# Loading the decay matrix's rows in two transfers, one for each half of a chunk

## Chip, cores and metric

The kernel runs on one core of one Trainium2 chip. The metric is device microseconds of one execution, the median of several runs.

## What is computed

The reference chains three parts. The first is a state-space layer: over chunks of the sequence, for each batch and head, it builds a lower triangular decay matrix L from the products of the decays a between two positions, multiplies it into C Bᵀ, applies the result to x, and adds what the running state contributes. The second and third are feed-forward networks over all 3072 tokens.

```python
for c in range(nc):
    cum = np.cumsum(la, axis=-1)
    L = np.exp(cum[:, :, :, None] - cum[:, :, None, :]) * causal
    M = np.einsum('bhin,bhjn->bhij', Cc, Bc) * L
    y_intra = np.einsum('bhij,bhjd->bhid', M, xc)
    y_inter = np.einsum('bhin,bhnd->bhid', Cc, state) * np.exp(cum)[:, :, :, None]
    y[:, :, sl] = y_intra + y_inter
    state = decay_full[:, :, None, None] * state + np.sum(Bx, axis=2)
...
h = x @ w_in                        # 256 -> 2048, then ELU, then w_out: 2048 -> 256
h = (x @ w1) * (x @ w2) @ w3        # 256 -> 1024
return h @ w_out
```

Shapes: batch 4, 8 heads, 768 positions, head size 32, state size 16; weights are float32.

## The kernel before

The tokens are cut in six tiles of 512 columns (t) and 24 chunks of 128 positions (k, four to a tile). A chunk is computed as two halves of 64 positions, SUB = 2 and R = 64; the two halves lie on partitions 0 to 63 and 64 to 127 of one tile.

For a chunk, `at_load` brings its inputs (xbc, 128 rows of 4 KB), `at_l` the decays for L, `at_prep` makes L with one scan on VectorE (line 333) and bd from its last column on GpSimd, `at_cb` multiplies C Bᵀ (cb) on TensorE and that into L on VectorE (line 357), `at_u` makes the state st, and `at_y` the output y, which is split into the high and low parts xT of the next layer. Chunks 0 to 3 get their decays by matmuls with a selection matrix (`at_wide`). From chunk 4 on, `at_l` loads them (line 310): the decays lie in device memory as a_cut, one row of 8 heads by 64 positions (2 KB) for each half chunk, and each row is broadcast to the 64 partitions of its half. L has three buffers; the loads run two to three chunks ahead.

A feed-forward matmul is done as three (`mm3`, lines 240 to 242) with high and low parts of both operands. Weights arrive as 64-bit words in pieces of 512 KB (raw_wi for w_in, raw_wo for w_out, raw_wq, raw_wc, raw_wa, raw_wb for the rest), and are turned into high and low parts by VectorE and ScalarE (lines 146 to 148, 103, 104). `unit_a` computes h and the activation e, then g; `unit_b` sums acc_b over w_out; `unit_w` folds w3 into the last weight; `unit_c` and `unit_d` do the second network. After `unit_b` of the first tiles x2 is spilled to device memory (x2_dram, line 493).

The order is set by a table at the start, by a planner's costs and due times afterwards, and by a scheduler of the framework that orders each engine's instructions. All transfers are issued by SP, in order. Eight completion semaphores (DMAHW0 to DMAHW7) are used in turn: a transfer waits until the one eight places before it has landed. VectorE, ScalarE and TensorE also take their instructions in order, so one that waits holds up those behind it.

Of the kernel before, what the change touches and what calls it, by code (L numbers as in the profile page):

```python
# [13 lines left out]
NB, NH, S, D, N = 4, 8, 768, 32, 16  # L14
Q = 128
SUB = 2
R = Q // SUB
# [26 lines left out]
def kernel(  # L44
# [20 lines left out]
    nc = tc.nc  # L65
# [191 lines left out]
    a_cut = tc.dram_tile([NCHUNK * SUB, NH, R], F32, name="a_cut")  # L257
# [48 lines left out]
    def at_l(k):  # L306
        c = ck[k]
        c["L"] = att.tile([P, NH, R], F32, tag="L", name=f"L{k}", bufs=3)
        if k >= CPT:
            nc.sync.dma_start(c["L"].rearrange("p h s -> p (h s)"),  # L310
                              a_cut[SUB * k:SUB * k + SUB].rearrange("s h (o i) -> s o (h i)", o=1)
                              .to_broadcast([SUB, R, NH * R]))

    def at_wide(k):

# [99 lines left out]
    def phases(k):  # L415
        t, first = k // CPT, k % CPT == 0

        def p0():
            if k >= CPT:
                with tc.issue_after(loads[-1]):  # L420
                    if first and t + 1 < NTILE:
                        at_pr(t + 1)
                    if k + LOADS - 1 < NCHUNK:
                        at_l(k + LOADS - 1)
                    if k + LOADS < NCHUNK:
                        at_load(k + LOADS)
            if first and t:
                at_decay(t)
            at_prep(k)

        def p1():
            at_cb(k)

        def p2():
            at_cd(k)
            at_u(k)

        def p3():
            at_y(k)

        return [p0, p1, p2, p3]
# [214 lines left out]
    for k in range(CPT):  # L656
        at_l(k)
# [4 lines left out]
    for j in ORDER:  # L662
# [6 lines left out]
        elif isinstance(j, tuple):  # L669
            i, stage = j  # L670
# [7 lines left out]
    for k in range(CPT, CPT + LOADS):  # L678
        if k < CPT + LOADS - 1:
            at_l(k)  # L680
        at_load(k)
# [67 lines left out]
```

## Time and profile before

| | |
|---|---|
| median of 3 runs | 588.4 us (588.01 to 589.73) |
| the profiled execution | 588.74 us, its span 587.0 us |
| TensorE (PE) busy | 560.5 us, 95% of the span |
| VectorE (DVE) busy | 336.2 us, 57% |
| ScalarE (ACT) busy | 277.7 us, 47% |
| GpSimd (POOL) busy | 83.8 us, 14% |
| transfers | 52.78 MB, 90 GB/s over the span |
| loads of L | 20 of 256 KB |

TensorE is busy nearly all the time, but not evenly: over the first 130 us or so it has gaps, and from there to the end almost none. The shares over the whole span therefore say little about a change to the loads of L, and the reading goes by stages: which engine is full in a stage, and what it waits for. An issue on SP is the time in which SP hands a transfer to its queue; the landing comes later. "DMA share" is the mean busy share of 16 DMA engines. "Granted clock" is TensorE's clock as a share of 2.4 GHz.

### The profile page before, as it was taken

To read this page: it belongs to the slowest core of one execution; us is meant where nothing else is said; L and a number is where in the kernel's file an instruction comes from. 1 tells how busy PE (TensorE), PEld (TensorE's weight loads), DVE (VectorE), ACT (ScalarE), POOL (GpSimd) and SP (SyncE) were. 2 spreads that over 40 slices of the span, in tenths; PEclk is the share of its full clock that TensorE was granted. 3 is DMA by queue.
4 is the path that set the end of the run, shared out by engine and by line. 5 is a ranking of instruction groups with operands and counts; after the bars stand their busy time and mean duration, and the time that the engine had idled before them with its cause. 6 is when DMAs were issued, how large, how long until landed. Compare 5 with 4: busy or idle time off the path is not lost.

```text
span 587.0 us, 10429 instructions
## 1 busy us (share of the span) xinstructions
PE 560.5 (95%) x4436; PEld 439.8 (75%) x4436; DVE 336.2 (57%) x468; ACT 277.7 (47%) x390; POOL 83.8 (14%) x91
## 2 busy tenths in 40 slices
PE   5986799999999999999999999999999999999996
PEld 3665577767877888887788787887777778888784
DVE  6697879677675865668433335343676353335332
ACT  2294567565564655775323223232454552355222
POOL 2201114322222312253000000000021000000000
PEclk9999699999999999999999999999999999999999
DMA  8885353724453331621013031100110000010000
GB/s 297 298 242 155 124 173 111 260 101 126 137 195 96 113 127 73 214 86 58 1 50 113 1 126 37 54 37 1 58 53 1 1 1 0 1 37 2 0 1 36
DMA packets 26567, 52.78 MB, mean 90 GB/s; under 512 B 1592, under 2 KB 9784, under 8 KB 26520
## 3 DMA queue, kind: packets, MB, share of 16 engines
q1 hardware_dynamic: 26520, 52.11, 27.1%
q8 instruction: 35, 0.57, 0.4%
q14 instruction: 12, 0.10, 0.1%
HBM read 45.71 MB, written 6.39 MB: 89 GB/s over the span
## 4 chain that ended last, share of the span: by engine, by line
PE 77%; DMA 10%; DVE 6%; ACT 2%; issue 2%; POOL 1%; SPq 0%; POOLq 0%; DVEq 0%; ACTq 0%
PE ab L240 8%; PE ab L241 7%; PE ab L242 7%; DMA L<-a_cut 6%; PE acc_b L240 6%; PE acc_b L241 6%; PE h L240 6%; PE acc_b L242 6%; PE h L242 5%; PE h L241 5%; PE acc_d L240 4%; PE acc_d L241 4%; PE acc_d L242 4%; PE y L405 2%; DMA raw_wc<-in_w3t 2%
## 5 line engine op out<-in xcount | busy, mean ns | idle before, releaser
L469 DVE SCALAR_TENSOR_TENSOR e<-e,h 128x1024 f32<-128x1024 f32 x48 | 58.4, 1216 | 39.8 <-ACT e L468 39.8
L241 PE MATMUL acc_b<-g,w_out_hi 128*128 128x512 f32 x192 | 77.3, 403 | 3.8 <-DVE g L104 3.8
L240 PE MATMUL acc_b<-g,w_out_lo 128*128 128x512 f32 x192 | 77.9, 406 | 3.1 <-DVE w_out_lo L104 2.1
L240 PE MATMUL h<-xTh,w_in_lo 128*128 128x512 f32 (+1 forms) x196 | 78.1, 399 | 1.9 <-DVE e L469 1.0
L104 DVE TENSOR_TENSOR g<-e,g 128x1024 fp32r<-128x1024 f32 x48 | 61.6, 1283 | 29.0 <-ACT g L103 28.7
L242 PE MATMUL h<-xTh,w_in_hi 128*128 128x512 f32 (+1 forms) x196 | 76.2, 389 | 0.0
L241 PE MATMUL h<-xTl,w_in_hi 128*128 128x512 f32 (+1 forms) x196 | 76.2, 389 | 0.0
L242 PE MATMUL acc_b<-g,w_out_hi 128*128 128x512 f32 x192 | 76.1, 396 | 0.0
L240 PE MATMUL ab<-x2h,w 128*128 128x512 f32 x192 | 74.6, 394 | 0.7 <-ACT x2h L103 0.7
L241 PE MATMUL ab<-x2l,w 128*128 128x512 f32 x192 | 75.0, 391 | 0.0
L103 ACT CAST g<-e 128x1024 fp32r<-128x1024 f32 x48 | 50.4, 1050 | 52.0 <-DVE e L469 38.1
L242 PE MATMUL ab<-x2h,w 128*128 128x512 f32 x192 | 74.8, 389 | 0.0
L466 ACT ACTIVATE e<-h 128x1024 f32<-128x1024 f32 x48 | 49.2, 1026 | 44.2 <-PE h L242 43.0
L514 DVE TENSOR_TENSOR pa<-pa,ab 128x512 f32<-128x512 f32 x48 | 32.6, 684 | 61.2 <-ACT pa L513 61.2
L513 ACT COPY pa<-ab 128x512 f32<-128x512 f32 x48 | 27.9, 589 | 74.4 <-PE ab L242 73.5
L104 DVE TENSOR_TENSOR p<-pa,p 128x512 fp32r<-128x512 f32 x48 | 32.9, 692 | 34.2 <-ACT p L103 33.8
L468 ACT ACTIVATE e<-e 128x1024 f32<-128x1024 f32 x48 | 51.0, 1063 | 0.9
L103 ACT CAST p<-pa 128x512 fp32r<-128x512 f32 x48 | 29.8, 622 | 44.9 <-PE acc_d L242 23.3
L366 POOL TENSOR_TENSOR cd<-xbc,pr 128x256 f32<-128x256 f32 x24 | 24.7, 1028 | 173.9 <-issue 85.8
L240 PEld LDWEIGHTS acc_b<-g,w_out_lo 128*128 128x128 f32 x192 | 36.6, 190 | 13.1 <-DVE w_out_lo L104 2.5
L241 PEld LDWEIGHTS acc_b<-g,w_out_hi 128*128 128x128 f32 x192 | 36.6, 191 | 12.8 <-DVE g L104 5.2
L240 PEld LDWEIGHTS h<-xTh,w_in_lo 128*128 128x128 f32 x196 | 37.2, 190 | 11.5 <-DVE e L469 1.5
(93 smaller groups left out, 898.5 us busy)
## 6 DMA issues: line engine op xcount, KB each, us to landing
xbc<-in_xc SPq DMA_DIRECT2D x24, 512.0 KB, 9.8
raw_wc<-in_w3t SPq DMA_DIRECT2D x16, 512.0 KB, 7.0
L<-a_cut SPq DMA_DIRECT2D x20, 256.0 KB
raw_wi<-in_w_in SPq DMA_DIRECT2D x8, 512.0 KB, 11.9
raw_wo<-in_w_out SPq DMA_DIRECT2D x8, 512.0 KB
out_t<-o SPq DMA_DIRECT2D x12, 256.0 KB, 2.0
raw_wq<-in_wo SPq DMA_DIRECT2D x4, 512.0 KB, 11.5
raw_wb<-in_w SPq DMA_DIRECT2D x4, 512.0 KB
```

What stands on the lines that cost most here:

```text
L103: A.copy(hi, raw)
L104: return lo_eng.tensor_tensor(out=lo, in0=raw, in1=hi.bitcast(F32), op=ALU.subtract)
L240: last_mm[:] = [T.matmul(out, wlo, xhi, start=first, stop=False, **kw).ins]
L241: T.matmul(out, whi, xlo, start=False, stop=False, **kw)
L242: T.matmul(out, whi, xhi, start=False, stop=last, **kw)
L366: G.tensor_tensor(out=c["cd"], in0=c["cp"].rearrange("p s (w i) -> p s w i", w=2), in1=c["pr"].rearrange("p s (o i) -> p s o i", o=1).to_b ...
L405: mm = T.matmul(both[rows, s, g], state[k, s][rows, D * g:D * g + D], c["cd"][rows, s, g], start=False, stop=True, skip_group_check=True)
L466: A.activation(e, h, AF.Exp)
L468: A.activation(e, e, AF.Relu, scale=-1.0, bias=1.0)
L469: V.scalar_tensor_tensor(out=e, in0=e, scalar=-1.0, in1=h, op0=ALU.mult, op1=ALU.max)
L513: A.copy(e, h[:, 0])
L514: V.tensor_tensor(out=e, in0=e, in1=h[:, 1], op=ALU.mult)
```

## The change

`at_l` issues two transfers for a chunk in place of one. Each brings the row of one half to its 64 partitions. In the one transfer the axes were half, partition, row; in each of the two they are partition and row, so that the partitions are outermost. Bytes, destination and source are the same.

```diff
--- before.py
+++ after.py
@@ -307,9 +307,10 @@
         c = ck[k]
         c["L"] = att.tile([P, NH, R], F32, tag="L", name=f"L{k}", bufs=3)
         if k >= CPT:
-            nc.sync.dma_start(c["L"].rearrange("p h s -> p (h s)"),
-                              a_cut[SUB * k:SUB * k + SUB].rearrange("s h (o i) -> s o (h i)", o=1)
-                              .to_broadcast([SUB, R, NH * R]))
+
+            for s in range(SUB):
+                nc.sync.dma_start(c["L"][R * s:R * s + R].rearrange("p h s -> p (h s)"),
+                                  a_cut[SUB * k + s:SUB * k + s + 1].rearrange("s h i -> s (h i)").to_broadcast([R, NH * R]))
 
     def at_wide(k):
```

SP has 20 transfers more, and the semaphores that go round are taken by other transfers. On SP, from the loads of L4 and L5 on (the number behind a name is the chunk or the piece), before:

```order
L310 DMA L4_430<-a_cut_86 128x1x512 [waits DMAHW3_49,DVE_49]
L310 DMA L5_434<-a_cut_86 128x1x512 [waits DMAHW4_49,DVE_49,PE_49]
L278 DMA xbc6_438<-in_xc 128x1024 [waits DMAHW5_49,Pool_49]
L136 DMA raw_wo3_357<-in_w_out 128x2x512 [waits DMAHW6_49,DVE_49]
L136 DMA raw_wi6_442<-in_w_in 128x2x512 [waits DMAHW7_49,DVE_49]
L136 DMA raw_wo4_465<-in_w_out 128x2x512 [waits DMAHW0_49,DVE_49]
L136 DMA raw_wi7_492<-in_w_in 128x2x512 [waits DMAHW1_49,DVE_49]
L136 DMA raw_wo5_519<-in_w_out 128x2x512 [waits DMAHW2_49,DVE_49]
L294 DMA pr2_537<-in_a_h 128x1x512 [waits DMAHW3_49,Pool_49]
L310 DMA L6_539<-a_cut_86 128x1x512 [waits DMAHW4_49,PE_49]
```

and now:

```order
L312 DMA L4_430<-a_cut_86 64x512 [waits DMAHW3_49,DVE_49]
L312 DMA L4_430<-a_cut_86 64x512 [waits DMAHW4_49]
L312 DMA L5_435<-a_cut_86 64x512 [waits DMAHW5_49,DVE_49,PE_49]
L312 DMA L5_435<-a_cut_86 64x512 [waits DMAHW6_49]
L278 DMA xbc6_440<-in_xc 128x1024 [waits DMAHW7_49,Pool_49]
L136 DMA raw_wo3_357<-in_w_out 128x2x512 [waits DMAHW0_49,DVE_49]
L136 DMA raw_wi6_444<-in_w_in 128x2x512 [waits DMAHW1_49,DVE_49]
L136 DMA raw_wo4_467<-in_w_out 128x2x512 [waits DMAHW2_49,DVE_49]
L136 DMA raw_wi7_494<-in_w_in 128x2x512 [waits DMAHW3_49,DVE_49]
L136 DMA raw_wo5_521<-in_w_out 128x2x512 [waits DMAHW4_49,DVE_49]
L294 DMA pr2_539<-in_a_h 128x1x512 [waits DMAHW5_49,Pool_49]
L312 DMA L6_541<-a_cut_86 64x512 [waits DMAHW6_49,PE_49]
```

L6 waited for DMAHW4, which L5 signals. Now its first half waits for DMAHW6, which the second half of L5 signals. xbc6 waits for DMAHW7 in place of DMAHW5.

Up to about the first fold of w3 the other engines have the order of before. There SP has, before:

```order
L310 DMA L11_1208<-a_cut_86 128x1x512 [waits DMAHW6_49,DVE_49,PE_49]
L278 DMA xbc12_1210<-in_xc 128x1024 [waits DMAHW7_49,Pool_49]
L493 DMA x2_dramh_87<-x2h0_1091 128x1024 [waits DMAHW0_49,Activation_49]
L136 DMA raw_wc1_1217<-in_w3t 128x4x256 [waits DMAHW1_49]
L493 DMA x2_draml_88<-x2l0_1092 128x1024 [waits DMAHW2_49,DVE_49]
L136 DMA raw_wc2_1221<-in_w3t 128x4x256 [waits DMAHW3_49,Pool_49]
```

and now:

```order
L312 DMA L11_1215<-a_cut_86 64x512 [waits DMAHW5_49,DVE_49,PE_49]
L312 DMA L11_1215<-a_cut_86 64x512 [waits DMAHW6_49]
L494 DMA x2_dramh_87<-x2h0_1098 128x1024 [waits DMAHW7_49,Activation_49]
L494 DMA x2_draml_88<-x2l0_1099 128x1024 [waits DMAHW0_49,DVE_49]
L278 DMA xbc12_1218<-in_xc 128x1024 [waits DMAHW1_49,Pool_49]
L136 DMA raw_wc1_1225<-in_w3t 128x4x256 [waits DMAHW2_49]
L136 DMA raw_wc2_1229<-in_w3t 128x4x256 [waits DMAHW3_49,Pool_49]
```

Both spills of x2 now stand before xbc12 and raw_wc1. On ScalarE, at the same place, before:

```order
L468 ACTIVATE e1_2_1201<-e1_2_1201 128x1024 [waits Activation_49]
L147 ACTIVATE raw_wc1_1217<-raw_wc1_1217 128x512 [waits DMAHW1_49,Pool_49]
L103 CAST g1_2_1205<-e1_2_1201 128x1024 [waits DVE_49,PE_49]
L103 CAST w3_1_1293<-raw_wc1_1217 128x512 [waits DVE_49]
L466 ACTIVATE e1_3_1271<-h1_3_1258 128x1024 [waits PE_49]
```

and now:

```order
L469 ACTIVATE e1_2_1208<-e1_2_1208 128x1024 [waits Activation_49]
L103 CAST g1_2_1212<-e1_2_1208 128x1024 [waits DVE_49,PE_49]
L147 ACTIVATE raw_wc1_1225<-raw_wc1_1225 128x512 [waits DMAHW2_49,Pool_49]
L467 ACTIVATE e1_3_1279<-h1_3_1266 128x1024 [waits PE_49]
L103 CAST w3_1_1301<-raw_wc1_1225 128x512 [waits DVE_49]
L469 ACTIVATE e1_3_1279<-e1_3_1279 128x1024 [waits Activation_49]
```

ScalarE takes the cast of g1_2 before raw_wc1 in place of after it. VectorE has a like exchange there.

## Rows read from the trace of the kernel before

**Rows 1.** Page, part 4: shares of the chain that ended last, by line.

```profile
PE ab L240 8%; PE ab L241 7%; PE ab L242 7%; DMA L<-a_cut 6%; PE acc_b L240 6%; PE acc_b L241 6%; PE h L240 6%; PE acc_b L242 6%; PE h L242 5%; PE h L241 5%; PE acc_d L240 4%; PE acc_d L241 4%; PE acc_d L242 4%; PE y L405 2%; DMA raw_wc<-in_w3t 2%
```

**Rows 2.** Chain of work from 15 to 75 us: start us, us, what.

```profile
19.86 21.72 DMA L<-a_cut
...
41.64 15.33 DMA L<-a_cut
...
64.44 0.43 PE acc_b L242
...
70.22 0.23 PE h L242
```

**Rows 3.** Busy us by stage: window, its length, PE PEld DVE ACT POOL, PEclk, DMA, GB/s.

```profile
28.00:53.00 25.00, 21.41 (x158) 16.05 (x159) 24.76 (x38) 20.19 (x29) 2.56 (x3) 1.00 0.74 214
57.00:65.20 8.20, 3.11 (x21) 2.35 (x22) 8.20 (x12) 4.65 (x7) 1.83 (x2) 0.59 0.48 163
66.90:80.00 13.10, 12.75 (x176) 9.35 (x175) 12.44 (x20) 5.62 (x8) 1.63 (x2) 0.93 0.50 152
106.00:122.00 16.00, 14.09 (x123) 9.91 (x122) 9.35 (x13) 8.12 (x9) 4.13 (x4) 1.00 0.77 266
122.00:260.00 138.00, 138.00 (x1206) 112.42 (x1205) 96.36 (x122) 84.88 (x119) 40.64 (x38) 1.00 0.37 124
```

**Rows 4.** Timeline of VectorE: start us, us, what, [idle before <-releaser].

```profile
52.44 0.68 DVE L104 TENSOR_TENSOR w_in_lo<-raw_wi,w_in_hi 128x512 fp32r<-128x512 f32 x1
57.00 1.22 DVE L333 TENSOR_TENSOR_SCAN L<-L,eye 128x512 f32<-128x512 f32 x1 [3.88 <-DMA L<-a_cut]
...
62.49 0.68 DVE L104 TENSOR_TENSOR w_out_lo<-raw_wo,w_out_hi 128x512 fp32r<-128x512 f32 x1
...
66.87 1.23 DVE L333 TENSOR_TENSOR_SCAN L<-L,eye 128x512 f32<-128x512 f32 x1 [1.64 <-DMA L<-a_cut]
```

**Rows 5.** Timeline of TensorE, same columns.

```profile
55.53 0.54 PE L405 MATMUL y<-cd,st 32*32 32x64 f32 x24
59.98 1.13 PE L351 MATMUL cb<-xbc 32*64 32x128 f32 x16 [3.91 <-issue]
63.22 0.79 PE L240 MATMUL acc_b<-g,w_out_lo 128*128 128x512 f32 x1 [2.11 <-DVE w_out_lo L104]
...
69.48 0.50 PE L240 MATMUL h<-xTh,w_in_lo 128*128 128x512 f32 x1
```

**Rows 6.** TensorE in one window: length, busy, granted clock, DMA share, GB/s.

```profile
58.00:60.00 2.00, 0.02 (x3) 0.61 0.93 308
```

**Rows 7.** DMA in two windows: length, PEclk, DMA share of 16 engines, GB/s.

```profile
17.00:18.00 1.00, 1.00 1.07 395
430.00:431.00 1.00, 1.00 0.13 51
```

**Rows 8.** Issues on SP: start us, us of issuing, what.

```profile
18.13 6.73 SPq L310 DMA_DIRECT2D L<-a_cut  x2
...
36.62 4.04 SPq L294 DMA_DIRECT2D pr<-in_a_h  x1
41.64 0.51 SPq L310 DMA_DIRECT2D L<-a_cut  x1
...
49.16 1.55 SPq L310 DMA_DIRECT2D L<-a_cut  x1
```

**Rows 9.** Waits from 106 to 122 us, by engine: us in total, times, longest.

```profile
DVE raw_wc L146 <- DMA raw_wc<-in_w3t: 3.1, 1, 3.1
ACT raw_wc L147 <- DMA raw_wc<-in_w3t: 4.4, 1, 4.4
PE acc_b L241 <- DVE g L104: 0.6, 1, 0.6
PE h L240 <- DVE e L469: 0.6, 1, 0.6
```

**Rows 10.** Chain of work at 105 us, columns as in rows 2.

```profile
104.81 10.60 DMA raw_wc<-in_w3t
```

## Prediction

> **What bounds the kernel now.** Start with the chain of work that ended last, because it names a transfer beside TensorE: the loads of L take 6% of the span, the other lines of that row are matmuls [rows 1]. In order of time the same chain shows where: a load of L lasts from 19.86 us for 21.72 us, directly behind it the next one lasts from 41.64 for 15.33 us, until 56.97 [rows 2], and at 57.00 VectorE begins the scan of L6 [rows 4]. A transfer of 256 KB that takes 15 us is the thing to explain, and so I read the DMA windows next. At 430 us a load of L is the only transfer in flight, and the 16 DMA engines are busy 0.13 of the time and move 51 GB/s; at 17 us, with 128-row transfers queued, they are busy all the time at 395 GB/s [rows 7]. 0.13 of 16 is two engines: the broadcast load, whose outermost axis is the 2 halves of the chunk, runs on two, 25 GB/s each, and 262,144 B need 5.1 us of them. Behind a full queue those two engines also hold up their share of every 512 KB transfer that follows.
>
> Then the issues on SP. The first two loads of L take 6.73 us to issue, the load of pr2 4.04 us, and the load of L6 goes out at 41.64 [rows 8], 0.06 us after L5 landed: in the order it waits for DMAHW4, the completion semaphore of L5, eight transfers back. So L6 is late because L5 is slow, not because its buffer is taken.
>
> Now what that costs. From 28 to 53 us VectorE is busy 24.76 of 25 us, from 57 to 65.2 all 8.20, from 66.9 to 80 12.44 of 13.1 [rows 3]; in between it stands twice for a load of L, 3.88 us before 57.00 and 1.64 us before 66.87 [rows 4]. VectorE sets the pace there, and these 5.52 us are its only sizeable gaps. TensorE idles behind it: 3.91 us before cb5, 2.11 us before acc_b for w_out_lo [rows 5], and in the window from 58 us its granted clock falls (mean 0.61), so that one matmul of 512 columns takes 0.43 us at the lower level, 1.2 GHz, against 0.23 us at 2.4 GHz [rows 2, 6].
>
> **The change part by part.** *Spread.* Each half has 64 rows as outermost axis, so I expect it on 16 engines. At 395 GB/s two halves need 0.66 us of all engines in place of 5.1 us of two; the bytes are the same. Suppose L5's second half goes out no sooner than both issues ended before, 18.13 + 6.73 = 24.9 us [rows 8]. At most eight transfers of 512 KB are in flight with it, 4.2 MB, 10.6 us at 395 GB/s: it lands by 35.5, no longer at 41.6.
>
> *L6.* Its first half still waits for a semaphore (DMAHW6, L5's second half), by then long given. SP reaches it when pr2 has been issued, 36.62 plus some 0.5 us, the length of an issue that nothing blocks [rows 8]. Ahead of it in the queue are raw_wi6, raw_wo4, raw_wi7, raw_wo5 and pr2, 2.4 MB; at 285 GB/s, an estimate between the 214 of the stage's mean [rows 3] and 395, that is 8.3 us. Had none of it begun by 36.6, L6 would land near 45 us; VectorE asks for it at 53.1, when w_in_lo is done [rows 4]. L7 goes out near 49 us as now [rows 8], lands near 54, and is asked for at 61.3. Both waits go: 3.88 + 1.64 = 5.5 us of VectorE.
>
> *What is late next.* VectorE starts L6 at 53.1 and reaches w_out_lo's end at 59.3 (63.2 less 3.9). TensorE has y done at 56.07, does cb5 at full clock to 56.7, and waits 2.5 us for w_out_lo: that wait stays, as it hangs on VectorE's order. If the clock now holds, its 12 matmuls take 2.8 us in place of 5.1, and h begins 6.4 us earlier than 69.48 [rows 5], which is more than VectorE's 5.5: VectorE sets it, gain **5.5 us**. If the clock falls again, the 12 matmuls take 5.1 us as before and TensorE is 3.9 to 4.1 us ahead: gain **4.0 us**. A pause of 3.91 us had the fall behind it, one of 2.5 us is not in the trace; pauses of 0.6 us [rows 9] have none, as the clock of their stage is 1.00 [rows 3]. I take the first, since the pause is shorter by more than a third, and keep the second for the range.
>
> *Added issues.* 20 more transfers on SP at about 0.5 us (an unblocked issue of L) are 10 us on a queue that computes nothing, and the 5 us issues go. Each also takes one of the eight semaphores, so fewer bytes can be in flight: xbc6 waits for pr1's load in place of raw_wi4's. xbc6 could go out only after 24.9 us, behind the blocked issues, so it should be no later. Priced at nothing; the cover is 8 us of slack on L6, and if it were gone each late us would fall on VectorE.
>
> *Order.* Up to the fold of w3 all engines keep their order. There SP has both spills of x2 ahead of xbc12 and raw_wc1, and VectorE and ScalarE take g and raw_wc1 in another order. Today raw_wc1 needs 10.60 us to land [rows 10], VectorE waits 3.1 and ScalarE 4.4 us for it, and TensorE pays 0.6 us twice [rows 9]. With L11 off the two engines it lands 4.5 us earlier; one 512 KB spill moved ahead and the wait for x2l take back 1.3 to 3 us. Bounds: a gain of 1.2 us (both bubbles gone) and a loss of 0.6 us (one more such bubble, since SP now holds xbc12 and raw_wc1 until VectorE has done x2l). I take a gain of **0.6 us**, nearer to the first, because the landing that both bubbles hang on moves forward on balance. From 122 to 260 us TensorE is busy all 138 us [rows 3], so what is won by then stays won, and nothing more is.
>
> Against that stands a rule of the Trainium skill (DMA: Bandwidth & Descriptors, Rules for kernel authors): of two transfers to disjoint partition halves it says "Don't bother", as both halves use the same 16 engines anyway, and one transfer of 128 partitions is better. By it the sum would be nothing, 588.7 us. The trace does not bear out its premise here: the one transfer has two engines, not 16 [rows 7].
>
> **Sum.** The profiled execution took 588.74 us, 1.7 us around its span of 587.0 and 0.3 us above the median. 588.7 - 5.5 - 0.6 = 582.6 us, and by the median 582.3 us.
>
> **The rivals.**
> *The clock falls again* (0.22): 588.4 - 4.0 - 0.6 = 583.8 us. For it: TensorE still stops for 2.5 us at the same place.
> *The split is no faster* (0.07): the halves run one after the other on few engines, or the source, still one row for each half, sets the engines. Each half then takes 2.6 us, L6 lands about as now: 588.4 us, within 0.5. Against it: transfers with 128 rows outermost get 395 GB/s together [rows 7]. The rule of the Trainium skill cited above would end in this rival.
> *The gain is given back at the fold* (0.10): raw_wc1 lands after VectorE asks, and TensorE pays two or three of the 0.6 us bubbles more, or a weight load that now comes sooner collides: 584.5 to 588 us.
> *The row itself is the limit, slower* (0.06): 16 engines now read one 2 KB row of a_cut at the same time; in the trace only one engine reads a row, at 25 GB/s. If a row gave no more than that to all, each half would hold all 16 engines 5.1 us, a chunk 10.3 us, and everything behind it waits. L4, L5 and L6 are 31 us of the queue, on top of the 10.6 us queued at 18 us and some 6.7 us of weights and xbc: L6 would land near 66 us in place of 57, about 598 us. The point where it decides is about 36 GB/s for a transfer: then L6 lands at 57 as now. I hold it unlikely, since two engines on neighbouring rows already get 51.
>
> **How the numbers follow.** My forecast, both waits gone and the clock held, has 0.55: 582.3 us. A run tells apart about 0.3%, 1.8 us, so faster means below 586.6. Faster: 0.55 + 0.22 + 0.09 of the fold case, with 0.02 off for late surprises, 0.84. Same: 0.07 + 0.01 + 0.01 = 0.09. Slower: 0.06 and 0.01 for what I have not seen, 0.07. For the range: below, 6.4 us (TensorE's bound at 69 us) and 1.2 us give 580.8, and I take 580.5; above, 4.0 us alone gives 584.4, and part of the fold case reaches 585.8.
>
> **What would show it.** Right: the DMA share while L is alone near 1 for under 1 us, not 0.13 for 5; no wait of VectorE's scan for L's load; SP issues of L at 0.5 us throughout; cb5 at about 56 us; VectorE without a gap from 28 to 75 us; the chain without L's loads. Whether the clock falls is read from the window of 58 to 60 us. Wrong: loads of L still on the chain, a DMA share of 1 at a low rate while L runs (the row limit), or TensorE's gaps from 106 to 122 us above the 1.9 us of now [rows 3].

## The result, and the profile after

The changed kernel took 582.8 us, median of four runs (581.79 to 583.48), against 588.51 us for the kernel before on the same chip: a ratio of 0.9897, 95% interval 0.9879 to 0.9916. The forecast was 582.3 us. In two later comparisons the ratio was 0.9916 (0.9900 to 0.9932) and 0.9880 (0.9858 to 0.9902). The profiled execution took 583.48 us, its span 581.7.

On the page the loads of L are gone from the chain that ended last, which answers to [rows 1]:

```profile
PE ab L240 8%; PE ab L241 7%; PE ab L242 7%; PE acc_b L240 6%; PE acc_b L241 6%; PE h L240 6%; PE acc_b L242 6%; PE h L242 5%; PE h L241 5%; PE acc_d L240 4%; PE acc_d L241 4%; PE acc_d L242 4%; PE y L406 2%; PE cb L352 2%; DMA raw_wb<-in_w 1%
```

The issues on SP, start and length in us [rows 8]. The row of the four halves of L4 and L5 lasts 5.17 us, but the issues in it take 0.44 to 0.51 us each; between them SP waits for the semaphores of weights still in flight. Before, the issue of L5 alone took 5.00 us. pr2 takes 0.66 in place of 4.04, and L6 goes out at 36.63 in place of 41.64:

```profile
18.55 5.17 SPq L312 DMA_DIRECT2D L<-a_cut  x4
25.07 0.35 SPq L278 DMA_DIRECT2D xbc<-in_xc  x1
...
35.88 0.66 SPq L294 DMA_DIRECT2D pr<-in_a_h  x1
36.63 1.11 SPq L312 DMA_DIRECT2D L<-a_cut  x2
...
46.71 1.39 SPq L312 DMA_DIRECT2D L<-a_cut  x2
```

VectorE begins the scans of L6 and L7 with no wait in brackets behind them, where there were 3.88 and 1.64 us [rows 4]:

```profile
52.29 1.21 DVE L334 TENSOR_TENSOR_SCAN L<-L,eye 128x512 f32<-128x512 f32 x1
...
60.44 1.21 DVE L334 TENSOR_TENSOR_SCAN L<-L,eye 128x512 f32<-128x512 f32 x1
```

TensorE in the same stretch [rows 5]. The wait before cb5 is gone. The wait for w_out_lo is there, 2.59 us; the distance of two matmuls behind it grows from 0.23 to 0.43 us, and h begins at 63.84, no longer at 69.48:

```profile
55.25 0.67 PE L352 MATMUL cb<-xbc 32*64 32x128 f32 x16
58.51 0.50 PE L240 MATMUL acc_b<-g,w_out_lo 128*128 128x512 f32 x1 [2.59 <-DVE w_out_lo L104]
58.84 0.40 PE L241 MATMUL acc_b<-g,w_out_hi 128*128 128x512 f32 x1
59.08 0.39 PE L242 MATMUL acc_b<-g,w_out_hi 128*128 128x512 f32 x1
...
62.00 0.63 PE L241 MATMUL acc_b<-g,w_out_hi 128*128 128x512 f32 x1
62.43 0.63 PE L242 MATMUL acc_b<-g,w_out_hi 128*128 128x512 f32 x1
...
63.84 0.50 PE L240 MATMUL h<-xTh,w_in_lo 128*128 128x512 f32 x1
```

Windows, with columns as in [rows 3]. From 60 to 62 us the granted clock is 0.50, which is 1.2 GHz. From 106 to 122 us TensorE is busy 15.09 us, before 14.09; TensorE is some 6 us ahead here, so this is not quite the same work, and in the window of the same work, 100.4 to 116.4 us, it is busy 14.44 us:

```profile
60.00:62.00 2.00, 2.00 (x6) 1.51 (x5) 2.00 (x4) 1.45 (x2) 0.00 (x0) 0.50 0.00 0
106.00:122.00 16.00, 15.09 (x163) 11.73 (x162) 12.20 (x18) 10.46 (x13) 2.51 (x3) 1.00 0.67 207
```

**Where the time went.** For each matmul I subtracted its start in the trace of before from the start of the matmul of the same name, and the same place in turn, in the trace of after; the median over 5 us of such differences is TensorE's shift, negative where it is ahead. From row 69.48 to row 63.84, for instance, it is -5.64. The shift has four steps: -0.75 us by 50 us, -5.64 at 80 us, -6.74 at 160 us, -5.60 from 280 us to the end. The first step comes before the first wait for L, and I do not count it as the change's: here TensorE's matmuls of 256 columns go over from 0.21 us apart to 0.12 at 25.5 us, in the kernel before at 28.7 us, while the granted clock of both stretches is noted as 1.00. The size of this step differs between profiles of one kernel, as the table below shows. So the change won 4.9 us where the waits for L were, 1.1 us at the fold of w3, and gave back 1.1 us near 260 us:

```profile
DVE raw_wa L146 <- DMA raw_wa<-in_w: 4.6, 2, 3.1
...
PE acc_b L241 <- DVE g L104: 1.9, 1, 1.9
```

These are the waits from 245 to 275 us (us in total, times, longest). Before, TensorE waited 0.8 us there for g. VectorE now stands 3.1 us for the last piece of w1, which the chain shows landing 6.38 us after its issue (253.14 6.38 DMA raw_wa<-in_w). Right behind that piece SP issues pr5, the two halves of L18 and xbc19.

### The profile page after: what moved, and what is told of

Its sections match the earlier page's. It is cut to its first block, busy times and chain, and to the rows that moved or that the text cites. A ratio compares the mean times of both kernels' runs of the same rounds, so it can differ in the third digit from the quotient of the medians.

```text
span 581.7 us, 10502 instructions
## 1 busy us (share of the span) xinstructions
PE 557.3 (96%) x4436; PEld 438.2 (75%) x4436; DVE 332.9 (57%) x468; ACT 277.8 (48%) x390; POOL 84.6 (15%) x91
## 4 chain that ended last, share of the span: by engine, by line
PE 78%; DVE 9%; DMA 5%; ACT 3%; issue 3%; POOL 1%; SPq 0%; DVEq 0%; POOLq 0%
PE ab L240 8%; PE ab L241 7%; PE ab L242 7%; PE acc_b L240 6%; PE acc_b L241 6%; PE h L240 6%; PE acc_b L242 6%; PE h L242 5%; PE h L241 5%; PE acc_d L240 4%; PE acc_d L241 4%; PE acc_d L242 4%; PE y L406 2%; PE cb L352 2%; DMA raw_wb<-in_w 1%
```

## The experiments

All kernels below are the changed kernel with one edit, except that after_again and after_third are the changed kernel itself. The table gives the time, the ratio to the kernel before, and the steps of TensorE's shift against the first profile of before: the shift at 50 us, and how much more TensorE was ahead (negative: behind) from 50 to 80 us, from 80 to 160 and from 160 to 280.

| kernel | us | ratio (95%) | at 50 us | L waits | fold | 260 us |
|---|---|---|---|---|---|---|
| changed | 582.8 | 0.9897 (0.9879 to 0.9916) | -0.75 | 4.9 | 1.1 | -1.1 |
| after_again | 583.6 | 0.9916 (0.9900 to 0.9932) | -0.26 | 6.0 | 0.9 | -0.1 |
| after_third | 583.1 | 0.9880 (0.9858 to 0.9902) | 1.26 | 6.0 | 1.3 | 0.0 |
| heads | 593.5 | 1.0060 (1.0043 to 1.0077) | -0.09 | -1.1 | -4.5 | 0.1 |
| only_4_7 | 583.4 | 0.9899 (0.9881 to 0.9917) | -0.46 | 6.0 | -0.3 | -0.1 |
| only_4_5 | 583.3 | 0.9897 (0.9872 to 0.9922) | 0.30 | 5.7 | -0.4 | -0.1 |
| from_8 | 588.1 | 0.9990 (0.9969 to 1.0012) | -0.43 | -0.7 | 1.6 | -1.1 |
| not_11 | 583.9 | 0.9922 (0.9906 to 0.9937) | -0.10 | 6.0 | -0.2 | -1.0 |
| not_18 | 582.2 | 0.9871 (0.9855 to 0.9888) | 1.38 | 6.0 | 1.6 | 0.0 |
| not_18_b | 581.7 | 0.9866 (0.9845 to 0.9886) | 0.02 | 6.0 | 1.6 | 0.0 |
| rows | 583.3 | 0.9894 (0.9864 to 0.9923) | 1.16 | 6.0 | 1.5 | -1.3 |
| fill | 584.0 | 0.9921 (0.9902 to 0.9941) | 1.38 | 4.4 | 1.3 | 0.1 |
| lo_pool | 584.7 | 0.9937 (0.9923 to 0.9952) | 1.24 | 3.4 | 2.6 | 0.0 |

### Spread or order: two transfers that stay on two engines

```diff
-            for s in range(SUB):
-                nc.sync.dma_start(c["L"][R * s:R * s + R] ...
+            for b in range(2):
+                nc.sync.dma_start(c["L"][:, 4 * b:4 * b + 4].rearrange("p h s -> p (h s)"),
+                                  a_cut[SUB * k:SUB * k + SUB, 4 * b:4 * b + 4].rearrange("s h (o i) -> s o (h i)", o=1)
+                                  .to_broadcast([SUB, R, 4 * R]))
```

> Two transfers for each chunk as in the changed kernel, but cut by heads (4 heads each), so that the outermost axis is still the 2 halves of the chunk: as many transfers, the same turn of the semaphores. Theory, the spread over 16 engines makes the gain: each transfer still has two engines (DMA share near 0.13 where one is alone), L5 lands near 41.6 us, VectorE waits some 3.9 us for L6 as before, and the time is 587 to 590 us. Rival, the later turn of the semaphores or the smaller transfers make it: L's loads leave the chain and the time is 582 to 584 us.

It took 593.5 us, above the theory's 590 and slower than before. VectorE's scans still wait for L, and SP stands 13.16 us over the first four issues, of which three take 2.7 to 5.6 us themselves. Where the last chunk's load is alone, it has a DMA share of 0.14 and 49 GB/s, as before [rows 7]:

```profile
19.90 13.16 SPq L312 DMA_DIRECT2D L<-a_cut  x4
```

```profile
438.00:439.00 1.00, 1.00 (x6) 0.84 (x5) 0.78 (x1) 0.00 (x0) 0.00 (x0) 1.00 0.14 49
```

```profile
58.25 1.23 DVE L335 TENSOR_TENSOR_SCAN L<-L,eye 128x512 f32<-128x512 f32 x1 [5.23 <-DMA L<-a_cut]
...
68.22 1.23 DVE L335 TENSOR_TENSOR_SCAN L<-L,eye 128x512 f32<-128x512 f32 x1 [1.74 <-DMA L<-a_cut]
```

The larger loss, 4.5 us, falls at the fold. Waits of VectorE and TensorE there, and then the window behind them, with the granted clock at 0.50:

```profile
DVE raw_wc L146 <- DMA raw_wc<-in_w3t: 4.3, 1, 4.3
...
PE y L407 <- DVE st L385: 2.3, 1, 2.3
...
PE h L240 <- DVE e L471: 1.4, 1, 1.4
```

```profile
124.00:128.00 4.00, 4.00 (x11) 3.08 (x10) 4.00 (x7) 1.91 (x4) 0.51 (x1) 0.50 0.59 196
```

This kernel has as many transfers, and the same turn of the semaphores, as the changed one; what it lacks is the spread. It differs in one thing more, its rows are 1 KB long in place of 2 KB; but alone its load moves 49 GB/s, where the kernel before has 51, so alone the shorter rows cost it nothing. So the spread makes the gain. The rival that the gain is given back at the fold is what two loads on two engines do there: raw_wc1 is late, TensorE stops for 2.3 and 1.4 us, and the clock falls to 1.2 GHz.

### Which chunks make which step

Two transfers for some chunks, the one transfer for the others; the edit is the condition:

```diff
+            if k < 8:          # only_4_7; k < 6: only_4_5; k >= 8: from_8
                 for s in range(SUB):
                     ...
+            else:
+                nc.sync.dma_start(c["L"].rearrange("p h s -> p (h s)"), ...
```

> Two transfers for chunks 4 to 7 alone, the one transfer for all later chunks. Theory, each step of the shift between the traces has its own chunks (4.9 us from L4 to L7 by 64 us, 1.1 us from L11 at the fold of w3 at 106 to 122 us, 1.1 us given back at 255 to 262 us where L18 is issued): the first stays, the second and third are not made, TensorE is 5 to 5.7 us ahead of the kernel before from 65 us to the end, and the time is about 583 us. Rival, the first loads carry only a part, and the loads of later chunks take back the other on two engines: 584.5 us or more.

> The one transfer for chunks 4 to 7, two transfers for all later chunks. Theory: VectorE waits for L6 and L7 at 57 and 67 us as in the kernel before (3.9 and 1.6 us), 1.1 us is won at the fold of w3 and 1.1 us given back at 255 to 262 us: 588 us, within 1. Rival, late loads of L cost the time too (they hold up the weights behind them all along): 586.5 us or less.

> Two transfers for chunks 4 and 5 alone. Theory, L6 was late because L5, whose semaphore it waits for, was slow on two engines: L6, one transfer, is issued at about 37 us and lands by 45, so the wait of 3.9 us goes; L7, one transfer, goes out at 47 us and needs some 8 us, so it lands before VectorE asks at 60 and that wait goes too: TensorE's lead at 80 us is 5 to 6 us, 583 to 584 us in all. Rival, L6 and L7 need the spread themselves: a wait of 1 to 4 us stays before either scan and the time is 585 to 587 us.

All three fit their theories. With L4 and L5 alone, L6 as one transfer goes out at 37.65 us with an issue of 0.54, and no scan waits:

```profile
37.65 0.54 SPq L316 DMA_DIRECT2D L<-a_cut  x1
...
47.76 0.51 SPq L316 DMA_DIRECT2D L<-a_cut  x1
```

```profile
53.34 1.21 DVE L339 TENSOR_TENSOR_SCAN L<-L,eye 128x512 f32<-128x512 f32 x1
...
61.48 1.21 DVE L339 TENSOR_TENSOR_SCAN L<-L,eye 128x512 f32<-128x512 f32 x1
```

L6 was therefore late because L4 and L5 were slow, by way of the semaphore and the blocked issues, and not by its own two engines. Two chunks of twenty carry nearly the whole gain (5.7 of 6.0 us). from_8 keeps both waits of VectorE (6.5 us in all, the longer 5.0) and ends at no change.

### The fold: one transfer for chunk 11

The same edit with `if k != 11`.

> Two transfers for all chunks but 11, which keeps the one; the order of SP at the fold of w3 (both spills of x2 ahead of raw_wc1) stays that of the changed kernel. Theory, the gain of 1.1 us at the fold comes from L11 on 16 engines, since raw_wc1, behind it in the queue, lands earlier: with L11 on two engines raw_wc1 lands 2 to 4 us later, VectorE waits for it again, and TensorE is 2 to 5 us later from 120 us on than in the changed kernel: 584.5 to 588 us. Rival, the new order makes the gain: nothing changes at the fold, and the time is 582.8 us.

It took 583.9 us. Its step at the fold is -0.2 us in place of the 0.9 to 1.3 of the changed kernel, so it loses 1.1 to 1.5 us there: the theory's sign, less than its 2 us. Waits of ScalarE and VectorE at the fold, first in the changed kernel, then with L11 in one transfer:

```profile
DVE raw_wc L146 <- DMA raw_wc<-in_w3t: 1.3, 1, 1.3
...
ACT raw_wc L147 <- DMA raw_wc<-in_w3t: 0.8, 1, 0.8
```

```profile
ACT raw_wc L147 <- DMA raw_wc<-in_w3t: 4.5, 1, 4.5
DVE raw_wc L146 <- DMA raw_wc<-in_w3t: 3.3, 1, 3.3
```

The second pair is that of before [rows 9] within 0.2 us. But the expectation was wrong on one point: with L11 in one transfer the order is that of before again. SP has raw_wc1 ahead of the second spill of x2, and ScalarE takes raw_wc1 before the cast of g:

```profile
97.47 0.42 SPq L278 DMA_DIRECT2D xbc<-in_xc  x1
98.04 0.34 SPq L499 DMA_DIRECT2D x_dramh<-x2h  x1
98.43 0.42 SPq L136 DMA_DIRECT2D raw_wc<-in_w3t  x1
100.85 0.33 SPq L499 DMA_DIRECT2D x_draml<-x2l  x1
```

So not_11 undoes the spread of L11 and the new order together and cannot tell them apart. (only_4_7 and only_4_5 have the order of before too, and steps of -0.3 and -0.4 us.) The kernel that helps is heads: both spills ahead of raw_wc1, and L11 on two engines:

```profile
105.15 0.83 SPq L495 DMA_DIRECT2D x_dramh<-x2h  x1
107.94 0.33 SPq L495 DMA_DIRECT2D x_draml<-x2l  x1
...
108.80 14.09 SPq L136 DMA_DIRECT2D raw_wc<-in_w3t  x5
```

There raw_wc1 lands 9.44 us after its issue, in the changed kernel 6.44, and heads loses 4.5 us at the fold where the changed kernel wins 0.9 to 1.3. So the new order without the spread does not make the gain. Whether L11 on 16 engines would make it in the order of before, no run shows.

### What is given back at 260 us: one transfer for chunk 18

The same edit with `if k != 18`, run twice, the second time beside the changed kernel.

> Two transfers for all chunks but 18, which keeps the one. Theory, L18's two transfers, issued at 254 us right behind the last pieces of w1, take from 16 engines what the last piece needs, so that it lands 6.4 us after its issue, VectorE waits 3.1 us for it and TensorE 1.9 us for g: with L18 on two engines the piece lands 1 to 3 us earlier, TensorE waits 0.8 us as in the kernel before, and the time is 1.1 us below the changed kernel, about 581.7 us. Rival, the piece is late because TensorE's gain makes all ask earlier for what a semaphore or a buffer releases no sooner: the wait of TensorE stays near 1.9 us and the time is that of the changed kernel, 582.8 us.

> Two transfers for all chunks but 18, beside the changed kernel. Theory: TensorE waits 0.8 us and not 1.9 us for g at 260 us in every execution, and the time is 0.3 to 1.1 us below the changed kernel's. Rival: no difference, and a wait of 1.9 us in this profile would show that L18's two transfers are not what makes the piece late.

> The changed kernel beside the kernel with one transfer for chunk 18. In three of six profiles of kernels with L18 in two transfers the last piece of w1 landed over 6 us after its issue and TensorE lost 1.1 us at 260 us; in none of two with L18 in one. Theory, L18 on 16 engines costs that in some executions: this kernel is 0.3 to 1.1 us slower than the other. Rival, the late piece is not of L18's making: no difference, both 582 to 583.5 us.

not_18 took 582.2 and 581.7 us, the changed kernel beside the second 583.1; the intervals of the two ratios (0.9845 to 0.9886 and 0.9858 to 0.9902) overlap. Both profiles of not_18 have the short waits, 0.8 us on TensorE. But so have after_again and after_third. VectorE's waits for w1 from 250 to 266 us, in not_18_b and then in from_8:

```profile
DVE raw_wa L146 <- DMA raw_wa<-in_w: 3.3, 2, 1.9
```

```profile
DVE raw_wa L146 <- DMA raw_wa<-in_w: 4.6, 2, 3.2
```

Over all profiles with L18 in two spread transfers, four of eight lost 1.0 to 1.3 us at 260 us (changed, from_8, not_11, rows) and four did not (after_again, after_third, fill, lo_pool); of five with L18 on two engines none did. That speaks for L18, which then shares the engines of the last piece of w1, but a loss in half the profiles is not enough to call it shown. It stays open what decides from one execution to the next.

### The clock

The column of the L waits shows another thing that differs between executions. Behind the same wait of 2.6 us for w_out_lo the clock fell to 0.50 in the first profile of the changed kernel, and it held at 1.00 in the eight other profiles that have that wait (the rows with 5.7 or 6.0).

> The changed kernel once more. In its first profile TensorE stood 2.6 us before the sums over w_out at 58.5 us and the granted clock fell behind it (0.50 from 60 to 63 us), while after the same 2.6 us it held in the profiles of two other kernels. Theory, whether the clock falls there differs from one execution to the next and moves the lead at 65 us between 4.9 us (fallen) and about 6.4 us (held): this profile shows one of the two, and the time is 582 to 583.5 us. Rival, the fall belongs to this kernel: it is there again, and the lead at 65 us is within 0.3 of 4.9 us from the stretch before it.

TensorE's window from 60 to 62 us in after_again, to be held against the one shown above:

```profile
60.00:62.00 2.00, 2.00 (x14) 1.38 (x17) 2.00 (x2) 0.97 (x2) 0.00 (x0) 1.00 0.00 0
```

With the clock held the step is 6.0 us, with the fall 4.9. The forecast's two cases are both real, and the first is the usual one. The six times of after_again spread from 582.06 to 584.67 us, by more than the 1.1 us between the two cases, so the clock there is not the only thing that varies.

Could the pause be filled, or removed?

```diff
+        if k == 5:
+            for _ in range(FILL):
+                T.matmul(cb[:, 1, 4 * R:], w_in_s[0][:, 0, :P], xT[0][0][:, 0, :4 * R], start=True, stop=True, skip_group_check=True)
```

> The changed kernel, with 20 matmuls of 256 columns into unused columns of cb5's accumulator behind cb5, so that TensorE works in the 2.6 us in which it waits for w_out_lo; they are extra work that no output uses. Theory: with no pause the granted clock stays 1.00 from 55 to 66 us, the 12 matmuls of acc_b take 0.23 us each, TensorE is 6.4 us or more ahead of the kernel before at 65 us, of which VectorE takes back some 0.4 by 80 us, and the time is about 1 us below an execution of the changed kernel with the fall: 581.5 to 582.5 us. Rival, the clock costs nothing here because VectorE sets the pace anyway: the lead at 80 us is that of the changed kernel, 4.9 us from the stretch before, and the time 582.8 us.

The 20 matmuls filled the gap (2.65 us) and the clock stayed at 1.00, but the step was 4.4 us, not 6.0. The experiment carried a cost of its own: VectorE's product of cb and L reads the accumulator that the extra matmuls write, and it now stands five instructions later on VectorE. In fill and then in after_third, which began the stretch alike:

```profile
64.86 0.68 DVE L362 TENSOR_TENSOR L<-cb,L 128x512 f32<-128x512 f32 x1
```

```profile
60.72 0.67 DVE L358 TENSOR_TENSOR L<-cb,L 128x512 f32<-128x512 f32 x1
```

TensorE waits for it (1.2 us before y). So this run tells nothing of what a held clock is worth; the profiles with the fall and without do.

```diff
     for p in queue[:first_n]:
         p.lo = V
+    for p in pc["w_out"][3:]:
+        p.lo = G
```

> The changed kernel, with the low parts of the last five pieces of w_out made on GpSimd in place of VectorE. VectorE makes one in 0.68 us, GpSimd the like in 1.53. Theory, VectorE sets the pace from 28 to 65 us: it is rid of 3.4 us of work, TensorE waits less than 2.6 us before acc_b at 58 us, and the lead at 80 us grows by 1 to 2 us: 581 to 582 us. Rival, GpSimd's low part comes later than VectorE's would, or VectorE's instructions beside it run longer than before: TensorE's wait stays or grows, 583 to 586 us.

The rival's time came, 584.7 us, but not by a late low part: TensorE's wait for it fell from 2.59 to 1.40 us, as the theory had it. GpSimd needs 2.07, 1.56 and 2.69 us for what VectorE does in 0.68, and beside its second one VectorE's scan of L7 takes 2.33 us in place of 1.21. TensorE then waits 1.59 us for xTl, which stands behind that scan on VectorE, and the granted clock is 0.50 from 66 to 69 us:

```profile
57.19 2.07 POOL L104 TENSOR_TENSOR w_out_lo<-raw_wo,w_out_hi 128x512 fp32r<-128x512 f32 x1 [0.17 <-ACT w_out_hi L103]
...
60.57 1.56 POOL L104 TENSOR_TENSOR w_out_lo<-raw_wo,w_out_hi 128x512 fp32r<-128x512 f32 x1 [0.16 <-ACT w_out_hi L103]
```

```profile
60.88 2.33 DVE L334 TENSOR_TENSOR_SCAN L<-L,eye 128x512 f32<-128x512 f32 x1
```

```profile
59.31 0.50 PE L240 MATMUL acc_b<-g,w_out_lo 128*128 128x512 f32 x1 [1.40 <-POOL w_out_lo L104]
...
63.91 0.32 PE L379 MATMUL u<-xbc,bd 64*32 64x64 f32 x8 [1.59 <-DVE xTl L104]
```

```profile
66.00:69.00 3.00, 3.00 (x8) 2.33 (x8) 3.00 (x7) 1.80 (x3) 1.12 (x1) 0.50 0.56 183
```

### Does one row, read by all engines, set a limit?

```diff
-                                  a_cut[SUB * k + s:SUB * k + s + 1].rearrange("s h i -> s (h i)").to_broadcast([R, NH * R]))
+                                  xc[0][R * s:R * s + R, :NH * R])
```

> The changed kernel, but every half of L is loaded from 64 different rows of 2 KB in device memory (the first chunk's input) in place of one row of a_cut 64 times: same bytes, partitions and order, wrong decays. While L is alone the changed kernel moved 270 to 287 GB/s at a DMA share of 0.76 to 0.79, and from 27 to 31 us, with L4 and L5 among what is in flight, 199 to 254 GB/s at a share of 1. Theory, engines that read one row at the same time wait for each other: from different rows L alone moves 350 GB/s or more of a full share, the stretch from 27 to 31 us 300 GB/s or more, and L5 lands some 2 us earlier; the time does not change by over 1 us, since L is not waited for. Rival, the many packets or the writes to 64 partitions set the rate: both rates stay within 10%.

The expectation's figures for L alone (270 to 287 GB/s) were misread by me: at 421.5 us the transfer in flight was a store of the output. L's own bytes move about 1.5 us after its issue. In the changed kernel and then in rows, a window of 1.5 us that begins there:

```profile
423.00:424.50 1.50, 1.50 (x9) 1.22 (x7) 1.50 (x2) 0.51 (x2) 0.34 (x2) 1.00 0.44 153
```

```profile
423.50:425.00 1.50, 1.50 (x8) 1.24 (x7) 1.50 (x2) 0.63 (x2) 0.34 (x2) 1.00 0.55 168
```

And from 27 to 31 us, in the changed kernel and in rows:

```profile
27.00:31.00 4.00, 3.63 (x21) 3.18 (x22) 3.66 (x9) 4.00 (x8) 0.00 (x0) 1.00 1.06 223
```

```profile
27.00:31.00 4.00, 3.51 (x33) 3.20 (x26) 3.00 (x8) 2.69 (x5) 0.00 (x0) 1.00 1.06 229
```

The rates are the same within 10%, so the theory fell: that 64 partitions get the same row costs little or nothing here.

## Why the prediction was right, point by point

*What bounds the kernel.* Right. Two engines for a load, the blocked issue of pr2, L6 behind L5's semaphore, two waits of VectorE: heads and only_4_5 show each link. L5's second half landed 9.9 us after its issue, at 33.1 (forecast by 35.5). L6 was issued at 36.6 (forecast 37.1); the chain shows its load for 7.77 us, to 44.4, and the longest landing among its halves is 9.6 us, at 46.2 (forecast near 45), 6 us before its scan. xbc6 was no later (25.07, before 24.96).

*The term for the waits: mis-sized.* "Both waits go: 3.88 + 1.64 = 5.5 us of VectorE" was right, the price was not: 6.0 us where the clock holds and 4.9 where it falls, in place of 5.5 and 4.0. The failing step is "which is more than VectorE's 5.5: VectorE sets it". I had taken VectorE as full from L7 on, but the stretch had slack, 12.44 of 13.1 us [rows 3]. With TensorE 6.4 us ahead at 66 us VectorE used that slack up; the same work in after_again:

```profile
60.30:73.50 13.20, 12.44 (x178) 9.32 (x177) 13.09 (x21) 7.31 (x10) 2.52 (x2) 1.00 0.47 152
```

and TensorE paid only 0.4 us of its lead, by 80 us. For the fall of the clock I had taken the twelve matmuls at 5.1 us, as before; they took 4.5 (58.51 to 62.99).

*The wait that stays.* Right: cb5 at 55.25 us (about 56), and 2.59 us for w_out_lo (2.5). *VectorE without a gap from 28 to 75 us* was wrong: in the first profile it waits 1.2 us for ScalarE at 68 us.

*The fold.* The sign was right and the size too small: 0.9 to 1.3 us in the changed kernel, up to 1.6 in from_8 and not_18, against 0.6 forecast with 1.2 as its upper bound. The mechanism, raw_wc1 landing sooner because L11 is off the two engines, fits: raw_wc1 lands 6.44 us after its issue, before 10.60, and heads, in the same order without the spread, loses. The loss that I set against it, from the new order, was not measured by itself, since no run has the spread in the order of before.

*"What is won by then stays won".* Wrong in the profiled execution, where 1.1 us went back near 260 us, and right in the next two. From 122 to 260 us TensorE had no gap [rows 3], and I took that for safety; but right behind that window it already waited 0.8 us for g in the trace of before, so VectorE and the last piece of w1 stood close behind it. That L18's two halves delay that piece is likely and not shown.

*The added issues.* Priced at nothing, and rightly: the loads of L cost 1.1 us of SP a chunk, with no wait of VectorE, ScalarE or TensorE for a transfer from 20 to 100 us.

*How the load looks alone.* Wrong: not a share near 1 for under 1 us, but about half of the engines for some 1.5 to 2 us; the two halves are issued 0.5 us apart. Nothing hung on it.

*The rivals.* The clock did fall again in the profiled execution, and held in after_again and after_third. By the rule of the Trainium skill (DMA: Bandwidth & Descriptors, Rules for kernel authors), that two transfers to disjoint partition halves are not worth making, the time would have stayed. The measurement decides otherwise here, where the one transfer has two engines and not the 16 of the rule's premise [rows 7]: 1.0% faster, while heads, two transfers that keep two engines, lost 0.6%. The limit by one row fell with rows. The gain given back at the fold did not happen here, but in heads it did, at 4.5 us.

That the number came so close is partly luck, because errors cancelled: 4.9 + 1.1 - 1.1 + 0.75 of the early step is 5.6 us in the first profile, where 6.1 were forecast; with the clock held and nothing given back the steps give 6.9 to 7.3.

The fastest medians are those of not_18 (582.2 and 581.7 us, ratios 0.9871 and 0.9866): faster than the kernel before, and below the changed kernel's three medians (582.8 to 583.6), though within its scatter.

## What to carry to other kernels

Look at the DMA share where a slow transfer is alone: 0.13 of 16 is two engines, and then the outermost axis of the transfer is worth more than its bytes. A slow transfer costs most through what stands behind it, blocked issues and the next turn of a semaphore: repairing the first two loads of twenty gave 5.7 of the 6.0 us won at the waits. Before saying that gains stay won because the leading engine has no gap, read how closely the next engine and its loads follow it.

## What the runs showed of the hardware that I had not expected

A DMA share of 1 does not mean full rate: 391 GB/s from 17 to 18 us and 223 from 27 to 31 us in the same trace, at shares of 1.04 and 1.06, and 229 in rows, where the loads of L read 64 different rows, so it is not that one row is read 64 times. What makes it is open.

```profile
17.00:18.00 1.00, 1.00 (x30) 0.71 (x22) 0.00 (x0) 0.28 (x2) 0.17 (x1) 1.00 1.04 391
```

The same kernel, with the same wait of 2.6 us at the same place, has TensorE's clock fall to 1.2 GHz behind it in one execution and not in another, 1.1 us apart; and the early step, where the matmuls' distance halves between 25 and 32 us, moves TensorE by -0.75 to +1.38 us between profiles, more than the gain at the fold that was to be measured here. The granted clock is noted as 1.00 on both sides of that step, so what makes it is not shown.
